# Attention scores of a batch in five PSUM jobs instead of six, with the plan of ten steps dealt anew, in a fused sparse-attention and mish kernel

## The chip, the cores and the metric

The kernel runs on 1 core of one Trainium2 chip. The metric is device time in microseconds (us), lower is better. The kernel before takes 282.59 us in the median of 3 runs (282.14 to 286.71). The execution that was profiled took 283.31 us, of which the profile's span covers 281.5 us.

## What is computed

Eight batches of 576 positions go through eight heads of 64 each, four with a local mask (the last 32 positions), four with a strided mask (every 32nd position back). The result, 4608 tokens by 512, then goes through two matrix products of 512x2048 and 2048x512 with a mish between them.

```python
scores = scale * np.matmul(q, k.transpose(0, 1, 3, 2))
mask_local = (rel >= 0) & (rel < stride)
mask_strided = (rel >= 0) & (pos[None, :] % stride == pos[:, None] % stride)
...
attn = attn / (np.sum(attn, axis=-1, keepdims=True) + 1e-09)
return np.matmul(attn, v).astype(np.float32)
...
h = x @ w_in
sp = np.where(h > 20.0, h, np.log1p(np.exp(np.minimum(h, 20.0))))
g = h * np.tanh(sp)
return (g @ w_out).astype(np.float32)
```

## The kernel before, in words

**The parts.** The tokens are taken in nine blocks of 512. From block 1 on, and for most of block 0's first product too, each matrix product is done as seven products of half size with sums of inputs and outputs (Strassen's way). A block's first product runs in four groups g of 512 features, each with the seven products `1:g` to `7:g` of four matmuls (128x128 weights, 256 columns); its second product has seven products in two halves each, `m1:0`, `m1:1` to `m7:1`, of eight such matmuls. Between them stand copies out of PSUM (`1c`, `5c`, `m1c`, `m5c`, `m6c`, `m4c`, on ScalarE when the word ends in A and on VectorE when it ends in D), VectorE's additions (`6c`, `7c`, `m3c`, `m7c`), the mish (`Z`, `E`, `H` on ScalarE), the input sums `x:0` to `x:3` (L115, tile xs, from tile xT) and the sums of the mish's output `n`, `g:1` to `g:3` (tile gs), all on VectorE.

**Attention.** A batch's scores come in units, 12 local ones (`l`, 96 queries by 128 keys) and 16 strided ones (`s`, 72 by 72), each for two inner indices e. Units are put together into jobs of two PSUM banks, one bank for each e: `q` computes the scores of a job (L261), `e` applies the exponential into SBUF (L264 to 271; one ACTIVATE where the two banks lie side by side, two where they don't), `k` multiplies by the mask on VectorE (L273), `v` multiplies by the values (L299) and `r` normalises (reciprocal and product, L304 to 318). Before the change there are three local jobs of 4 units and three strided ones of 6, 6 and 4 (L230, L231), each in a pair of banks of its own.

**PSUM.** Eight banks: SET0 and SET1 of two banks, EE0 and EE1 of one, AT of two. Blocks take SET and EE by turns for the two products; attention uses AT ("A" in the plan's words), EE0 with EE1 ("G"), or one bank of a SET with an EE ("F", "H").

**What sets the order.** Nothing is scheduled by a tool: ten strings of words, PLANS (L732 to 833), are walked from left to right (`do`, L621; `go`, L728), and each engine gets its instructions in the order in which the words issue them. So a word's place sets its place in the queue of its engine alone. Semaphores make an instruction wait for what it reads and for the readers of what it overwrites. `@b` names a batch; `^` and `_` in front of a word mean the next and the last block. Step t (one string) does block t's first product, block t-1's second, and the attention of batch t+1. Step 0 also starts up: loads, attention of batches 0 and 1, and block 0 in plain products (`p1`, `p2`, matmuls of 512 columns).

**Transfers.** GpSimd's queue issues the loads (`ld`), and words `hold` (L683) make it wait until a transposing DMA has landed. SyncE's queue issues the transposing DMAs: `D` (q and k of a batch, from batch 3 on), `y` (the local half of the attention's result into xT, L321) and `V`, and the stores `st` and `w`. Batches 0 to 2 are transposed on TensorE instead (`T`, L199) and copied by `t`; `X`, `Y` and `xc`, `yc` do the same for the result.

## Time and profile before

| | |
|---|---|
| median of 3 runs | 282.59 us |
| profiled execution | 283.31 us |
| its span | 281.5 us |
| step 0 (start, loads, batches 0 and 1) | 0 to 56.0 us of the span |
| step 1, step 2 | to 75.2, to 102.6 us |
| steps 3, 4, 5, 6 | to 132.1, 160.7, 189.6, 216.9 us |
| steps 7, 8, 9 (no attention left) | to 242.5, 265.2, 277.5 us |
| granted TensorE clock | 1.00 throughout |

How to read it: a profile row of a timeline has start, time, engine, source line, operation, tiles written and read, shape and count, and in brackets the idle time of the engine before it and what ended that. PE is TensorE's matmul side, PEld its weight loads, ACT is ScalarE, DVE VectorE, POOL GpSimd; SPq and ACTq are queues that issue DMAs. Matmuls follow each other before the earlier ones end, so a row of eight lasts longer than eight times their spacing, and TensorE's loss shows in the distance between starts rather than in its busy share.

### The profile page before, as it was taken

The page shows a single profiled execution, that of the slowest core. Times are in us where ns is not written, and L with a number is a line of the kernel's source. Part 1 is how long each engine was busy: PE and PEld are TensorE (multiplying, and loading weights), DVE is VectorE, ACT ScalarE, POOL GpSimd, SP SyncE. Part 2 cuts the span into 40 slices and gives each one's busy share as a digit, 9 for nine tenths or more (in the row PEclk, how much of TensorE's full clock was granted, in tenths as well). Part 3 has the DMA queues.
Part 4 walks back from the last instruction along what each step waited for, and adds up shares of the span by engine and source line. Part 5 has one row for each costly group of instructions (what it writes and reads, how often), then busy time and mean ns, then how long its engine had stood idle before and what let it go on. Part 6 is the DMA issues. An engine that isn't in the chain of part 4 may idle for free.

```text
span 281.5 us, 7627 instructions
## 1 busy us (share of the span) xinstructions
PE 273.5 (97%) x3235; PEld 226.1 (80%) x3241; DVE 225.4 (80%) x384; ACT 186.1 (66%) x288; POOL 57.2 (20%) x78
## 2 busy tenths in 40 slices
PE   8899999999999999999999999999999999999994
PEld 3656845679888887889898888898989888888883
DVE  4679878899899895999789969889889957837761
ACT  2575984699777787569766986679488217624830
POOL 8533421250019005400720072001000000000000
PEclk9999999999999999999999999999999999999999
DMA  7999999999929978999899899998444003002104
GB/s 148 182 205 203 204 185 191 131 229 117 169 45 118 138 140 172 194 127 160 165 194 130 164 194 166 122 154 200 62 165 68 9 2 149 2 3 98 53 0 149
DMA packets 98242, 37.35 MB, mean 133 GB/s; under 512 B 79800, under 2 KB 93688, under 8 KB 98208
## 3 DMA queue, kind: packets, MB, share of 16 engines
q0 software_dynamic: 57808, 18.30, 63.3%
q1 hardware_dynamic: 40112, 18.32, 29.2%
q8 instruction: 25, 0.41, 0.6%
q10 hardware_dynamic: 288, 0.25, 0.3%
q14 instruction: 9, 0.07, 0.1%
HBM read 37.05 MB, written 9.44 MB: 165 GB/s over the span
## 4 chain that ended last, share of the span: by engine, by line
PE 86%; DMA 6%; DVE 3%; ACT 2%; POOL 1%; issue 1%; SPq 0%; ACTq 0%; DVEq 0%; POOLq 0%
PE set L121 52%; PE ee L121 20%; PE at L121 7%; PE at L299 4%; DMA vl<-in_v_dram 4%; DMA qTs<-qs 2%; PE at L346 1%; PE ee L346 1%; DVE xs L115 1%; DVE wos L115 0%; DVE gs L115 0%; DVE osb L112 0%; DVE xT L112 0%; ACT gT L450 0%; ACT Pl L269 0%
## 5 line engine op out<-in xcount | busy, mean ns | idle before, releaser
L121 PEld LDWEIGHTS <-wis 128*128 128x128 bf16 x577 | 55.7, 99 | 10.7 <-issue 2.4
L121 PEld LDWEIGHTS <-gs 128*128 128x128 bf16 x512 | 49.0, 98 | 6.7 <-issue 0.5
L121 PEld LDWEIGHTS <-gT 128*128 128x128 bf16 x448 | 42.1, 98 | 9.4
L121 PEld LDWEIGHTS <-w_in 128*128 128x128 bf16 x436 | 40.7, 97 | 7.3 <-DMA w_in<-in_moe_w_in_dram 0.7
L121 PE MATMUL set<-w_out,gT 128*128 128x256 bf16 (+1 forms) x299 | 46.1, 294 | 0.2
L121 PE MATMUL set<-xT,w_in 128*128 128x256 bf16 (+1 forms) x263 | 40.2, 275 | 0.4 <-ACT gT L450 0.2
L450 ACT ACTIVATE gT<-set 128x1024 bf16<-128x1024 f32 x32 | 32.8, 1025 | 8.9 <-PE set L121 8.5
L121 PE MATMUL set<-xs,wis 128*128 128x256 bf16 x256 | 38.4, 273 | 0.0
L110 ACT COPY set<-set 128x512 f32<-128x512 f32 x35 | 20.2, 576 | 16.3 <-PE set L121 14.9
L121 PE MATMUL set<-wos,gs 128*128 128x256 bf16 x224 | 28.0, 273 | 0.0
L115 DVE TENSOR_TENSOR hh<-set,hh 128x512 f32<-128x512 f32 x32 | 21.9, 685 | 5.3 <-PE set L121 4.9
L115 DVE TENSOR_TENSOR ee<-set,hh 128x512 f32<-128x512 f32 x32 | 22.3, 696 | 3.8 <-PE set L121 1.7
L448 ACT ACTIVATE gT<-hh 128x512 bf16<-128x512 f32 x35 | 22.0, 635 | 4.0 <-DVE hh L115 3.7
L115 DVE TENSOR_TENSOR gs<-gT,gs 128x2048 bf16<-128x2048 bf16 x16 | 19.5, 1220 | 3.6 <-ACT gT L448 1.8
L446 ACT ACTIVATE gT<-ee 128x512 bf16<-128x512 f32 x35 | 20.1, 595 | 2.0 <-PE ee L121 2.0
L121 PE MATMUL ee<-xs,wis 128*128 128x256 bf16 x140 | 20.9, 273 | 0.0
L121 PE MATMUL ee<-xT,wis 128*128 128x256 bf16 x140 | 20.8, 272 | 0.0
L110 ACT COPY hh<-ee 128x512 f32<-128x512 f32 x20 | 11.7, 585 | 12.5 <-PE ee L121 12.5
L115 DVE TENSOR_TENSOR gs<-gT 128x2048 bf16<-128x2048 bf16 x16 | 19.5, 1218 | 0.2 <-ACT gT L448 0.2
L316 DVE TENSOR_TENSOR x_s<-at,rden 72x768 bf16<-72x768 f32 (+1 forms) x22 | 18.8, 856 | 0.8
L121 PE MATMUL set<-xs,w_in 128*128 128x256 bf16 x128 | 19.2, 272 | 0.0
L121 PE MATMUL ee<-wos,gT 128*128 128x256 bf16 x128 | 16.1, 273 | 0.0
(145 smaller groups left out, 453.0 us busy)
## 6 DMA issues: line engine op xcount, KB each, us to landing
out_dram<-osb SPq DMA_DIRECT2D x17, 512.0 KB, 3.8
vl<-in_v_dram POOLq DMA_DIRECT2D x8, 288.0 KB, 12.6
w_out<-in_moe_w_out_dram POOLq DMA_DIRECT2D x4, 512.0 KB, 15.2
ks<-in_k_dram POOLq DMA_DIRECT2D x7, 288.0 KB, 11.6
qs<-in_q_dram POOLq DMA_DIRECT2D x7, 288.0 KB, 10.3
vraw<-in_v_dram POOLq DMA_DIRECT2D x7, 288.0 KB, 7.3
w_in<-in_moe_w_in_dram POOLq DMA_DIRECT2D x3, 512.0 KB, 15.5
kl<-in_k_dram POOLq DMA_DIRECT2D x10, 144.0 KB, 9.6
```

The source lines that it names most:

```text
L110: Sc.copy(out_, in_)
L115: eng.tensor_tensor(out=out_, in0=a, in1=b, op=op)
L121: PE.matmul(o, lhsT=lhsT, rhs=rhs, start=start, stop=stop, skip_group_check=True)
L299: PE.matmul(po[:, e, i, :] if kind == "l" and self.apart else po[:, (n - n0) // per, (n - n0) % per, :], lhsT=pt[0:r, c0:c0 + 128], rhs=rh ...
L316: Dv.tensor_tensor(out=xo, in0=po[0:m, :, :, 0:D], in1=rd.unsqueeze(3).to_broadcast([m, nb, per, D]), op=ALU.mult,)
L346: PE.transpose(tr[:, n * j:n * j + n], x[0:n, u:u + 2, :].rearrange("p u d -> p (u d)"), ident[0:n, 0:n],)
L446: Sc.activation(o[:, 0:2, 256:512], two(E), AF.Mish)
L448: Sc.activation(o[:, 2:4, 256:512], two(h[:, 1, :]), AF.Mish)
L450: Sc.activation(o[:, :, 0:256].rearrange("p (b u) n -> p b u n", b=2), pair[:, 0:2, :].rearrange("p b (u n) -> p b u n", u=2), AF.Mish,)
```

## The change

The jobs of a batch are cut otherwise: strided 2, 7 and 7 units, local 5, 5 and 2. A new function `first` gives the first strided job an offset of two local units, so that the job of 2 strided units and the job of 2 local units can stand side by side in one pair of banks (columns 0 to 191 and 192 to 335 of each). From batch 2 on they do, and the batch's scores take five pairs instead of six; batches 0 and 1 keep six. The exponential keeps one call for each of the two small jobs. The sizes of the SBUF tiles and their cleared tails follow. The strings of PLANS are all written anew from the point in step 0 where batch 0's attention ends: the same words in other places, 18 of them moved from ScalarE to VectorE and 21 the other way. The rows of GpSimd's and SyncE's queues keep their order.

```diff
-    P_s = [sb([PN, 2, n * PN + 56], f"Ps{i}") for i, n in enumerate((6, 6, 4))]
-    P_l = [sb([128, 2, n * WQ + 32], f"Pl{i}") for i, n in enumerate((4, 4, 4))]
+    P_s = [sb([PN, 2, n * PN + 56], f"Ps{i}") for i, n in enumerate((2, 7, 7))]
+    P_l = [sb([128, 2, n * WQ + 32], f"Pl{i}") for i, n in enumerate((5, 5, 2))]
...
-                "s": [S_UNITS[0:6], S_UNITS[6:12], S_UNITS[12:16]],
-                "l": [L_UNITS[0:4], L_UNITS[4:8], L_UNITS[8:12]],
+                "s": [S_UNITS[0:2], S_UNITS[2:9], S_UNITS[9:16]],
+                "l": [L_UNITS[0:5], L_UNITS[5:10], L_UNITS[10:12]],
...
+        def first(self, kind, i):
+            return 2 * WQ if kind == "s" and i == 0 else 0
+
...
-            o = 0
+            o = self.first(kind, i)
             for x, y in self.parts[kind][i]:
...
-            o = len(self.parts[kind][i]) * (WQ if kind == "l" else PN)
+            c, o = len(self.parts[kind][i]) * (WQ if kind == "l" else PN), self.first(kind, i)
...
-                Sc.activation(pt[0:n, :, 0:o], ps[0:n, :, 0:o], AF.Exp, scale=scale)
+                Sc.activation(pt[0:n, :, 0:c], ps[0:n, :, o:o + c], AF.Exp, scale=scale)
...
-                "m1:1 m1c:A g:1 ae g:2 m5:0 m2:0 x:0 q:l0:A e:l0:A q:l1:F m2:1 m6:0 e:l1:F q:s0:F e:s0:F sh:D q:l2:A "
+                "g:1 m5:0 _Z:3 m5:1 m1c:D _xc:1:A:A@3 m6:0 q:l0:A q:l1:F x:0 m2:0 m2:1 _st:1 ae _ld:kl@5 e:l1:F sh:A "
```

What that moves, at three places.

ScalarE in step 3, from the table load ahead of the exponentials of batch 4 to the last of them (Pl is a local job, Ps a strided one; at_106 is the pair A, set0_102 with ee0_104 the pair F). Before:

```order
L688 ACT_TABLE_LOAD
L271 ACTIVATE Pl0_88<-at_106 128x2x384
L269 ACTIVATE Pl1_89<-set0_102 128x384
L269 ACTIVATE Pl1_89<-ee0_104 128x384
L269 ACTIVATE Ps0_85<-set0_102 72x432
L269 ACTIVATE Ps0_85<-ee0_104 72x432
L271 ACTIVATE Pl2_90<-at_106 128x2x384
L269 ACTIVATE Ps2_87<-set0_102 72x288
L269 ACTIVATE Ps2_87<-ee0_104 72x288
L271 ACTIVATE Ps1_86<-at_106 72x2x432
```

With the change:

```order
L691 ACT_TABLE_LOAD
L272 ACTIVATE Pl1_89<-set0_102 128x480
L272 ACTIVATE Pl1_89<-ee0_104 128x480
L110 COPY vl0_79<-vl0_79 32x4x5x64
L274 ACTIVATE Pl0_88<-at_106 128x2x480
L274 ACTIVATE Ps0_85<-at_106 72x2x144
L274 ACTIVATE Pl2_90<-at_106 128x2x192
L272 ACTIVATE Ps2_87<-set0_102 72x504
L272 ACTIVATE Ps2_87<-ee0_104 72x504
L274 ACTIVATE Ps1_86<-at_106 72x2x504
```

The first strided job went from the pair F to the pair A beside the last local one, its exponential stands ahead of that one's, and the copy of shared values (`sh`) came from VectorE to ScalarE.

VectorE in step 3, around the sums x:1 and x:2 (xs read from xT; xT's local half is written by the DMAs `y`), g:3 (gs) and m7c (osb). Before:

```order
L277 TENSOR_TENSOR Pl1_89<-Pl1_89,consts_sb_72 128x2x384
L115 TENSOR_TENSOR xs_63<-xT_62,xs_63 128x512
L115 TENSOR_TENSOR xs_63<-xT_62 128x512
L115 TENSOR_TENSOR gs_64<-gT_71,gs_64 128x2048
L115 TENSOR_TENSOR osb_1970<-set1_103,o5_66 128x2x256
L277 TENSOR_TENSOR Ps0_85<-Ps0_85,consts_sb_72 72x2x432
```

With the change:

```order
L115 TENSOR_TENSOR gs_64<-gT_71,gs_64 128x2048
L280 TENSOR_TENSOR Pl1_89<-Pl1_89,consts_sb_72 128x2x480
L280 TENSOR_TENSOR Pl0_88<-Pl0_88,consts_sb_72 128x2x480
L280 TENSOR_TENSOR Ps2_87<-Ps2_87,consts_sb_72 72x2x504
L115 TENSOR_TENSOR osb_1951<-set1_103,o5_66 128x2x256
L280 TENSOR_TENSOR Ps1_86<-Ps1_86,consts_sb_72 72x2x504
L280 TENSOR_TENSOR Pl2_90<-Pl2_90,consts_sb_72 128x2x192
L115 TENSOR_TENSOR xs_63<-xT_62 128x512
L115 TENSOR_TENSOR xs_63<-xT_62,xs_63 128x512 x2
```

The two sums stood ahead of g:3 and m7c; now they stand five rows behind m7c's masks, and m7c has no row that reads xT ahead of it since x:0.

TensorE at the two ends of block 0's second product. Its first matmuls (p2, 128x512), before:

```order
L208 MATMUL at_106<-consts_sb_72,kl_75 64x96
L121 LDWEIGHTS gT_71
L121 MATMUL set1_103<-w_out_59,gT_71 128x512
L121 LDWEIGHTS gT_71
L121 MATMUL set1_103<-w_out_59,gT_71 128x512
```

and with the change:

```order
L208 MATMUL at_106<-consts_sb_72,kl_75 64x96
L121 LDWEIGHTS gT_71
L121 MATMUL set0_102<-w_out_59,gT_71 128x512
L121 LDWEIGHTS gT_71
L121 MATMUL set0_102<-w_out_59,gT_71 128x512
```

The first rows of 512 columns go to SET0 now, the pair that group 3's mish (Z:3) has just read; before they went to SET1. And the first matmul of step 1's product 1:0, also into SET0, before:

```order
L121 MATMUL set1_103<-qTs_83,kTs_84 128x72
L121 LDWEIGHTS kTs_84
L121 MATMUL ee1_105<-qTs_83,kTs_84 128x72
L121 LDWEIGHTS w_in_58
L121 MATMUL set0_102<-xT_62,w_in_58 128x256
```

and with the change:

```order
L208 MATMUL ee1_105<-consts_sb_72,kl_75 64x96
L121 LDWEIGHTS w_in_58
L121 MATMUL set0_102<-xT_62,w_in_58 128x256
L121 LDWEIGHTS kTl_82
L121 MATMUL set1_103<-qTl_81,kTl_82 128x96
```

A job of scores (the six-unit s0) stood between the last transpose and 1:0; now 1:0 follows the transposes at once and the first score job, l0, comes behind it.

More of the change, by code (lines that the diff above doesn't have):

```diff
@@ L236, in __init__ @@
             }
+        def first(self, kind, i):
+            return 2 * WQ if kind == "s" and i == 0 else 0
         def bias(self, kind, i, ps):
-            nu = len(self.parts[kind][i])
+            nu, o = len(self.parts[kind][i]), self.first(kind, i)
             m, w, bm = (128, WQ, loc_b) if kind == "l" else (PN, PN, stm_b)
@@ L242, in bias @@
                 mm(
-                    (ps[e] if isinstance(ps, tuple) else ps[:, e])[:, 0:nu * w].rearrange("p (u c) -> p u c", u=nu), ident[0:m, :],
+                    (ps[e] if isinstance(ps, tuple) else ps[:, e])[:, o:o + nu * w].rearrange("p (u c) -> p u c", u=nu), ident[0:m, :],
                     bm.unsqueeze(1).to_broadcast([m, nu, w]), True, False,
@@ L268, in exp @@
                 for e in range(2):
-                    Sc.activation(pt[0:n, e, 0:o], ps[e][0:n, 0:o], AF.Exp, scale=scale)
+                    Sc.activation(pt[0:n, e, 0:c], ps[e][0:n, o:o + c], AF.Exp, scale=scale)
             else:
-                Sc.activation(pt[0:n, :, 0:o], ps[0:n, :, 0:o], AF.Exp, scale=scale)
+                Sc.activation(pt[0:n, :, 0:c], ps[0:n, :, o:o + c], AF.Exp, scale=scale)
         def mask(self, kind, i, meng):
@@ L603, in clear @@
             Dv.memset(kTs[:, 16 * SU:], 0.0)
-            for p, n in zip(P_s, (6, 6, 4)):
+            for p, n in zip(P_s, (2, 7, 7)):
                 Dv.memset(p[:, :, n * PN:], 0.0)
             Dv.memset(kTl[:, 0:32], 0.0)
-            for p in P_l:
-                Dv.memset(p[:, :, 4 * WQ:], 0.0)
+            for p, n in zip(P_l, (5, 5, 2)):
+                Dv.memset(p[:, :, n * WQ:], 0.0)
         def plain1(fc, to, ccs):
@@ L740 @@
                 "sh:D@0 b:l1:A@0 q:l1:A:b@0 X:0:e@0 e:l1:A@0 q:l0:C:b@0 wi:1536:2048 xc:0:e:D@0 ld:ks@1 X:1:f@0 "
[16 rows of a table removed]
-            ),
-            (
[6 rows of a table removed]
-            ),
-            (
[10 rows of a table removed]
-            ),
-            (
[8 rows of a table removed]
-            ),
-            (
[8 rows of a table removed]
-            ),
-            (
[7 rows of a table removed]
-            ),
-            (
[7 rows of a table removed]
-            ),
-            (
[5 rows of a table removed]
-            ),
-            (
[4 rows of a table removed]
-            ),
-            (
-                "m1:1 m1c:1:D _3:3 _E:3 m1c:0:D m5:0 m5:1 _4:3 g:1 m6:0 g:2 m6:1 _Z:3 m2:0 m5c:A m6c:1:D m7:1 m6c:0:A "
-                "m7c:1 g:3 m2:1 z:b:A w:b:S m3:1 m7:0 m7c:0 m3:0 m3c m4:1 m4:0 z:0:A z:1:A st:1 w:0:S w:1:A "
[15 rows of a table added]
+            ),
+            (
[7 rows of a table added]
+            ),
+            (
[9 rows of a table added]
+            ),
+            (
[8 rows of a table added]
+            ),
+            (
[8 rows of a table added]
+            ),
+            (
[7 rows of a table added]
+            ),
+            (
[7 rows of a table added]
+            ),
+            (
[5 rows of a table added]
+            ),
+            (
[4 rows of a table added]
+            ),
+            (
+                "m1:1 _H:3 m1c:0:D m5:0 _4:3 m5:1 _2:3 _Z:3 g:1 m1c:1:D m6:1 g:2 m6:0 m5c:D m3:1 m2:0 m6c:0:D m6c:1:D "
+                "g:3 m7:0 _st:0 m7:1 _st:1 m2:1 z:b:A w:b:S m7c:1 m3:0 m7c:0 m4:0 m4:1 m3c z:0:A st:1 w:0:S z:1:A "
+                "w:1:A "
             ),
```

139 rows, old and new, of the table PLANS are left out of this document.

## The prediction

> **What bounds the kernel now.** I read the page's busy table first, then the chain that ended last, then busy time by step. The page's first table and its chain:
>
> ```profile
> PE 273.5 (97%) x3235; PEld 226.1 (80%) x3241; DVE 225.4 (80%) x384; ACT 186.1 (66%) x288; POOL 57.2 (20%) x78
> PE 86%; DMA 6%; DVE 3%; ACT 2%; POOL 1%; issue 1%; SPq 0%; ACTq 0%; DVEq 0%; POOLq 0%
> ```
>
> TensorE is busy for all but 281.5 - 273.5 = 8.0 us, and the chain is TensorE for 86%. Busy time by step (the columns are from:to, length, PE, PEld, DVE, ACT, POOL, then the granted clock, the DMA share and GB/s), for steps 2 to 5 and 7:
>
> ```profile
> 75.20:102.60 27.40, 27.40 (x361) 24.12 (x360) 25.89 (x44) 21.05 (x33) 7.44 (x9) 1.00 1.02 109
> 102.60:132.10 29.50, 28.85 (x358) 25.10 (x355) 24.86 (x41) 21.40 (x34) 7.12 (x10) 1.00 1.26 160
> 132.10:160.70 28.60, 28.60 (x358) 24.98 (x355) 24.58 (x41) 21.36 (x33) 7.10 (x9) 1.00 1.25 167
> 160.70:189.60 28.90, 28.90 (x351) 25.34 (x348) 24.70 (x41) 21.50 (x32) 7.12 (x9) 1.00 1.34 158
> 216.90:242.50 25.60, 25.60 (x236) 22.86 (x234) 19.17 (x29) 11.95 (x19) 0.00 (x0) 1.00 0.18 54
> ```
>
> In each TensorE is full while VectorE and ScalarE have room (step 2's VectorE least, 1.5 us). How full is full, the chain in order of time says:
>
> ```profile
> 143.07 2.62 PE set L121 x24
> ```
>
> 2.62/24 = 0.109 us for a matmul of 256 columns; a half (8) is 0.87, a product (4) 0.44. The change adds and removes no matmul of that kind, no transfer and no score: same words, other places. So it can take only from TensorE's waits, and add others. The waits are few, and one step holds the largest. Steps 3 and 4 run the same list of words in the plan of before, yet take 29.5 and 28.6 us; step 3, in order of time:
>
> ```profile
> 106.69 1.04 PE L121 MATMUL set<-wos,gs 128*128 128x256 bf16 x8
> 107.97 0.27 PEld L121 LDWEIGHTS <-kTs 64*128 64x128 bf16 x12 [0.53 <-issue]
> 108.00 0.19 PE L121 MATMUL set<-qTs,kTs 64*128 64x72 bf16 x1 [0.28 <-DMA qTs<-qs]
> 111.74 0.43 DVE L115 TENSOR_TENSOR xs<-xT,xs 128x512 bf16<-128x512 bf16 x1 [1.02 <-issue]
> 112.42 1.22 DVE L115 TENSOR_TENSOR gs<-gT,gs 128x2048 bf16<-128x2048 bf16 x1
> 113.39 0.53 PE L299 MATMUL at<-vl,Pl 128*128 128x65 bf16 x12
> 113.55 0.68 DVE L115 TENSOR_TENSOR osb<-set,o 128x512 f32<-128x512 f32 x1
> 114.29 0.93 PE L121 MATMUL set<-w_out,gs 128*128 128x256 bf16 x7 [0.37 <-DVE osb L115]
> ```
>
> TensorE could have gone on at 106.69 + 8 x 0.109 = 107.56 and starts q:s0 at 108.00, when the transposed queries land: 0.44. Then it waits again: v:l0's last matmul starts 0.19 before the row's end, the next could come at 113.75, and m4:0 starts at 114.29, after m7c (the osb row): 0.54. m7c is late because x:1 sat ahead of it on VectorE, idle 1.02 us. What x:1 reads, the profile of tile xT shows:
>
> ```profile
> L323 SPq DMA_TRANSPOSE xT<-x_l x2: 1267/1567/1867, 105.4 to 107.3; - x2
> DMA to landing us min/median/max: 3.2/3.8/4.3
> ```
>
> the second of the pair is issued at 107.3 and lands up to 4.3 later, 111.6, just before x:1 starts. Both waits have a transfer behind them and come in this step alone: in step 4 the DMAs have caught up.
>
> **The change part by part.** *Step 3: -0.98.* Between q:l0 and q:s0 stood m2:1 and m6:0; now m2:0, m2:1, m6:1 and m3:1, and three halves precede q:l0 instead of two (from m1 on): q:s0 comes 3 x 0.87 = 2.6 us later in TensorE's work, the transfer was 0.44 late. The two DMA queues keep their order, and what starts them (r:l1 of batch 2, behind m1c, r:l0 and g:1 as before) too, so it lands when it did. And m7c no longer stands behind x:1. The gain is 0.44 + 0.54 = 0.98. What is late next is x:1 itself, now ahead of 6:0: from m7:1 VectorE has m7c 0.68, two masks, x:2 and x:1, some 2.4 by the rows; TensorE has 5:0, 1:0, v:l0 and m4, 0.87 + 0.36 + 1.75 = 2.98. Covered by 0.5. Bounds: nothing to 0.98.
>
> *Step 0, product 1:3: -0.34.* The mish Z:1, then TensorE:
>
> ```profile
> 27.44 1.02 ACT L450 ACTIVATE gT<-set 128x1024 bf16<-128x1024 f32 x1 [1.36 <-PE set L121]
> 27.91 0.43 PE L202 MATMUL at<-consts_sb,ks 72*128 72x72 bf16 x8 [0.51 <-DMA ks<-in_k_dram]
> 28.51 0.60 PE L121 MATMUL set<-xT,w_in 128*128 128x256 bf16 x4 [0.17 <-ACT gT L450]
> ```
>
> The eight transposes take about 0.26 (0.43 less the last one's 0.17 of pipeline), so TensorE stood from 28.17 to 28.51: 0.34. Now T:ks0 (0.26) and 7:2 (0.44) stand between; 0.70 covers it. The 0.51 ahead of the transposes is a load that lands at 27.9 either way, so whatever the new order gains or loses between 21 and 27.9 (yc:0 now stands behind three sums on VectorE, up to 0.5) ends there: priced at nothing, at most 0.3 beyond it.
>
> *p2:0:0 behind Z:3: +0.45.* Before, Z:3 and the last transposes:
>
> ```profile
> 34.28 0.70 PE L208 MATMUL ee<-consts_sb,ql 96*64 96x96 bf16 x24
> 34.45 1.02 ACT L450 ACTIVATE gT<-set 128x1024 bf16<-128x1024 f32 x1
> ```
>
> Z:3 starts 0.17 after the transposes begin and takes 1.02, and nobody needed its banks. Now p2:0:0 does, after three groups of transposes. A group costs 0.26 (0.70 less 0.17 for two), three 0.78 and the switch about 0.1. Z:3 also waits for 2:3 now, and its end is 0.27 + 1.02 + 0.04 = 1.33 behind 2:3: 1.33 - 0.88 = 0.45. Bounds: 0.2 to 1.1 (no cover at all).
>
> *1:0 and q:l0 of step 1 behind oc:0: +0.57.* The copy of block 0's output and the two copies of queries behind it:
>
> ```profile
> 54.90 0.45 PE L208 MATMUL ee<-consts_sb,kl 96*64 96x96 bf16 x12
> 55.11 1.22 DVE L112 COPY osb<-set 128x1024 f32<-128x1024 f32 x1
> 56.24 1.41 DVE L112 COPY qTl<-at 128x576 bf16<-128x576 bf16 x2
> 56.42 0.61 PE L121 MATMUL set<-xT,w_in 128*128 128x256 bf16 x4
> ```
>
> oc:0 begins 0.21 after the transposes and ends at 1.43. Before, four groups of transposes and a score job filled 54.90 to 56.42, 1.52 us: no loss. Now four groups alone, 4 x 0.26 + 0.11 = 1.15, and 1:0 waits 1.43 + 0.06 - 1.15 = 0.34. Behind it q:l0 needs the first copy of queries, 1.43 + 0.7 = 2.16 after the start, and TensorE is there at 1.49 + 0.44 = 1.93: 0.23 more. Bounds: 0.2 to 1.0.
>
> *v:s2 behind r:s1 in steps 3 and 4: -0.24.* In step 3 before:
>
> ```profile
> 125.56 0.95 DVE L316 TENSOR_TENSOR x_s<-at,rden 72x768 bf16<-72x768 f32 x1
> 126.01 0.60 PE L121 MATMUL set<-xT,w_in 128*128 128x256 bf16 x4
> 126.57 0.40 PE L299 MATMUL at<-vs,Ps 72*128 72x65 bf16 x8
> ```
>
> 1:3 leaves TensorE free at 126.45, r:s1 ends at 126.51, v:s2 starts at 126.57: 0.12 lost, with three products between v:s1 and v:s2. Now there are four (0.44 more). Twice 0.12.
>
> *The tail: -0.28.* The last two halves, their copies and stores:
>
> ```profile
> 275.73 1.91 PE L121 MATMUL at<-w_out,gs 128*128 128x256 bf16 x16
> 277.67 0.65 ACT L110 COPY osb<-at 128x256 f32<-128x256 f32 x2 [3.78 <-PE at L121]
> 278.07 0.35 SPq L563 DMA_DIRECT2D out_dram<-osb  x1
> 278.35 0.37 ACTq L563 DMA_DIRECT2D out_dram<-osb  x1
> ```
>
> m4:1 came before m4:0, and z:0, first on ScalarE, waited for the last half; so both copies run after it. Now m4:0 is first, its copy runs under m4:1, and the last store leaves one copy's step earlier, 278.35 - 278.07.
>
> *The rest: nothing.* Five jobs instead of six change neither columns nor matmuls. The exponentials' cost by the rows
>
> ```profile
> L271 ACT ACTIVATE Pl<-at 128x768 bf16<-128x768 f32 x13 | 10.5, 808 | 2.4 <-PE at L121 2.2
> L269 ACT ACTIVATE Pl<-ee 128x384 bf16<-128x384 f32 x13 | 6.0, 492 | 1.1 <-PE ee L121 1.1
> ```
>
> is (808 - 492)/384 = 0.82 ns a column and 0.18 us fixed. From batch 3 on a batch has eight calls instead of nine, 0.18 us of ScalarE, which has 6 us of room a step. The runs of score jobs, at whose ends TensorE loses about 0.1, number 30 in both orders. Counting the other handoffs of steps 1 to 9 in both orders, I find some wider and some narrower, and take zero; bounds -1.2 (what TensorE loses there now) to +2.5 (five steps with a new wait of 0.5, as long as step 3's).
>
> The sum: -0.98 - 0.34 + 0.45 + 0.57 - 0.24 - 0.28 = -0.82. Against its own time the profiled execution would go from 283.31 to 282.5; it ran 0.72 above the median of the runs, and against the median of 282.59 the forecast is **281.8 us**.
>
> A rule that speaks against the change is in the Trainium skill, page "PSUM — Partial Sum Buffer", section "PSUM bank collisions raise a hardware error": two engines must not touch one bank (in the same quadrant) at once, so a guard belongs on the bank, not on the address. For the shared pair this means that l2's exponential may not start under q:s0's matmuls although their columns differ. ScalarE's new order meets it by putting s0's exponential first. By the rule l2's exponential starts a short call later, some 0.3 us by the rows above; without it, at once; the sum is -0.82 by both, as long as ScalarE is on time. No run here shows the collision.
>
> **The rivals.** *B, the gains without the new waits.* If the two new waits fall under others (Z:3 and oc:0 earlier, since their engines were relieved) the sum is -0.98 - 0.34 - 0.24 - 0.28 = -1.84, and with half of the 1.2 of small waits 282.59 - 2.44 = 280.2. For it: the rest of the plan was dealt anew as well. Against: oc:0's chain is plain arithmetic on four rows.
>
> *C, nothing is gained.* The DMA loop of steps 2 to 5 (loads, four transposes, hold) or a later wait takes up what step 3 gives; only the order changed. 282.6. Against it: step 4 with the same words is 0.9 us shorter than step 3.
>
> *D, slower: the shared pair on a late ScalarE.* q:s1 needs the pair A again after both small exponentials: 0.41 (288 columns) + 0.49 less an overlap of 0.1, and 0.1 of handoff, 0.9 us, where TensorE has one half and q:s2, about 1.1. Before, one call of 0.81 stood there. From 0.2 us of lateness on, TensorE waits. In step 3 `sh` is now in ScalarE's way, whose price as the row of step 0 gives it is
>
> ```profile
> 44.75 1.26 ACT L110 COPY vl<-vl 32x1280 bf16<-32x1280 bf16 x1 [1.19 <-DMA vl<-in_v_dram]
> ```
>
> With half of that lost in each of steps 2 to 6, 5 x 0.63 = 3.2 comes on top: 281.8 + 3.2 = 285.0, slower than before. Against it: between q:l0 and q:l2 TensorE has 3.5 us now instead of 1.9, and VectorE took m1c and m5c off ScalarE there.
>
> **How the numbers follow.** The forecast has 0.48, B 0.22, C 0.13, D 0.12, and 0.05 is left for a wait that I don't see. The range 279.9 to 284.3 us takes in C, B with nearly all of the small waits gone (282.59 - 1.84 - 0.85), and the forecast with the rest at its upper bound (281.8 + 2.5); most of D and the unseen are outside. Two per cent, about what a measurement of this kernel can tell from no change, is 5.7 us: under 276.9 nothing in the profile could pay for, since TensorE is idle for 8.0 us in all and most of that is start and end; faster 0.02. Above 288.2 lies the far end of D and most of the unseen: slower 0.05. Within 2%: 0.93.
>
> **What would show it.** Right: step 3 as long as step 4, q:s0 without a wait for qTs, m4:0 without a wait for osb; p2:0:0 starting with ScalarE's gT row as its releaser and 1:0 with DVE's osb row; the last two copies apart, one under the last half. Wrong: a wait of TensorE at q:s1 for ScalarE's Pl row in each of steps 2 to 6 (D), the same distance from step start to q:s0's transfer as before but a new wait behind it (C), or TensorE's waits between 34 and 58 us no longer than before (B).

## The result, and the profile after

The change makes the kernel slightly slower: 285.13 us in the median of 22 runs, where the kernel before takes 283.06 on the same chip; the ratio is 1.0072, 95% interval 1.0051 to 1.0093. The forecast was 281.8, so it had the wrong sign. The runs also scatter more: 283.1 to 286.7 us for the change, 282.1 to 283.7 for the kernel before. (Executions in which the chip lowered the clock or stretched the start count in the medians, but are left out of the ranges of runs and of every ratio, and the profiles of e17 and e18 are of such ones.) The profiled execution took 284.39 us, its span is 282.6, against 283.31 and 281.5 before.

The page's first table and its chain after the change:

```profile
PE 273.8 (97%) x3241; PEld 227.0 (80%) x3241; DVE 223.6 (79%) x381; ACT 189.4 (67%) x286; POOL 57.5 (20%) x78
PE 84%; DVE 6%; DMA 5%; POOL 2%; issue 1%; ACT 1%; DVEq 0%; ACTq 0%; POOLq 0%
```

TensorE is as full as before, but VectorE has 6% of the chain instead of 3%. Where that lies shows when the steps are compared at equal work. The words at a step's end differ, so the starts of the steps are set right by what crosses them (m1:0 and m1:1 are 0.87 us of TensorE each, v:l0 is 0.36, 4:3 0.44):

| stretch | change against before, us | forecast |
|---|---|---|
| steps 0 and 1 | +0.97 | +0.68 |
| step 2 | +0.16 | 0 |
| step 3 | -1.05 | -1.10 |
| step 4 | -0.14 | -0.12 |
| step 5 | +0.01 | 0 |
| step 6 | +1.12 | 0 |
| steps 7 to 9 and the tail | +0.01 | -0.28 |
| sum | +1.08 | -0.82 |

Without step 6 the changes cancel: what step 3 gives, steps 0 to 2 take.

First what came as forecast. Step 3 in order of time, the rows that answer to those of before (the halves m2:0 and m2:1, the hold that waits for the transposed queries, the first strided scores, m7c, v:l0 and m4):

```profile
107.89 1.92 PE L121 MATMUL set<-w_out,gT 128*128 128x256 bf16 x16
108.87 0.18 POOL L689 COPY hold<-qTs 1x2 bf16<-1x2 bf16 x1 [17.06 <-DMA qTs<-qs]
111.58 0.23 PE L121 MATMUL at<-qTs,kTs 64*128 64x72 bf16 x4
114.37 0.69 DVE L115 TENSOR_TENSOR osb<-set,o 128x512 f32<-128x512 f32 x1
115.05 0.53 PE L302 MATMUL at<-vl,Pl 128*128 128x65 bf16 x12
115.41 1.80 PE L121 MATMUL set<-w_out,gs 128*128 128x256 bf16 x15
```

The transposed queries land 0.9 us later than before (the hold wakes at 108.87 instead of 108.01), but q:s0 comes at 111.58 and waits for nothing; m7c ends as v:l0 starts, and m4 follows without an idle bracket. Both waits of 0.44 and 0.54 are gone.

The new waits of steps 0 and 1, p2:0:0 behind Z:3, then 1:0 behind oc:0 and q:l0 behind the copies, are where the prediction put them:

```profile
34.48 1.02 ACT L453 ACTIVATE gT<-set 128x1024 bf16<-128x1024 f32 x1 [0.39 <-PE set L121]
35.56 1.02 PE L121 MATMUL set<-w_out,gT 128*128 128x512 bf16 x4 [0.28 <-ACT gT L453]
56.88 0.60 PE L121 MATMUL set<-xT,w_in 128*128 128x256 bf16 x4 [0.17 <-DVE osb L112]
57.41 0.38 PEld L121 LDWEIGHTS <-kTl 64*128 64x128 bf16 x10 [0.21 <-ACT kTl L110]
```

From start to start TensorE loses 0.45, 0.34 and 0.23 us at them. Two more were not forecast, product 4:2 behind 7c:2 and product 7:0 of step 1 behind 6c:0, 0.46 and 0.36 from start to start:

```profile
30.02 0.60 PE L121 MATMUL set<-xs,w_in 128*128 128x256 bf16 x4 [0.30 <-DVE hh L115]
61.82 0.60 PE L121 MATMUL set<-xs,wis 128*128 128x256 bf16 x4 [0.20 <-DVE ee L115]
```

Then step 6, VectorE and the first local product with the values of batch 7 (vc:1 is the first copy xT from ks, which holds the strided result brought by the transposing DMA V; sh is the copy vl):

```profile
188.31 1.91 SPq L332 DMA_TRANSPOSE ks<-x_s  x1
194.04 0.72 DVE L112 COPY xT<-ks 128x576 bf16<-128x576 bf16 x1 [2.33 <-DMA ks<-x_s]
196.38 0.71 DVE L112 COPY xT<-ks 128x576 bf16<-128x576 bf16 x1
198.49 1.22 DVE L115 TENSOR_TENSOR gs<-gT,gs 128x2048 bf16<-128x2048 bf16 x1
200.07 0.48 DVE L112 COPY vl<-vl 32x1280 bf16<-32x1280 bf16 x1
200.61 0.46 PE L302 MATMUL at<-vl,Pl 128*128 128x65 bf16 x10 [1.24 <-DVE vl L112]
```

VectorE stands 2.33 us for V, everything behind vc:1 in its queue comes later, sh last, and v:l0 stops after two matmuls for 1.4 us from start to start. The rows of before have the same transfer and no wait:

```profile
187.31 1.95 SPq L329 DMA_TRANSPOSE ks<-x_s  x1
195.11 0.71 DVE L112 COPY xT<-ks 128x576 bf16<-128x576 bf16 x1
```

V landed at 191.8 there and the copy came 3.3 us later. That is one wait in one execution, and it accounts for the profile's 1.1 us; the median lies 2 us above. The experiments look for the rest.

### The profile page after: what moved, and what is told of

Its sections match the earlier page's. It is cut to its first block, busy times and chain, and to the rows that moved or that the text cites. A ratio compares the mean times of both kernels' runs of the same rounds, so it can differ in the third digit from the quotient of the medians.

```text
span 282.6 us, 7628 instructions
## 1 busy us (share of the span) xinstructions
PE 273.8 (97%) x3241; PEld 227.0 (80%) x3241; DVE 223.6 (79%) x381; ACT 189.4 (67%) x286; POOL 57.5 (20%) x78
## 4 chain that ended last, share of the span: by engine, by line
PE 84%; DVE 6%; DMA 5%; POOL 2%; issue 1%; ACT 1%; DVEq 0%; ACTq 0%; POOLq 0%
PE set L121 51%; PE ee L121 20%; PE at L121 7%; DMA w_in<-in_moe_w_in_dram 5%; PE at L302 4%; DVE xs L115 1%; DVE wis L115 1%; PE at L349 1%; DVE wos L115 1%; POOL w_in L173 0%; PE ee L349 0%; DVE qTl L112 0%; DVE ee L115 0%; DVE osb L112 0%; POOL vl L160 0%
## 5 line engine op out<-in xcount | busy, mean ns | idle before, releaser
L121 PE MATMUL set<-wos,gs 128*128 128x256 bf16 x224 | 27.6, 273 | 0.0
L110 ACT COPY set<-set 128x512 f32<-128x512 f32 x31 | 17.9, 579 | 9.0 <-PE set L121 8.1
L110 ACT COPY osb<-set 128x1024 f32<-128x1024 f32 (+1 forms) x8 | 7.7, 960 | 15.8 <-PE set L121 15.8
L110 ACT COPY hh<-ee 128x512 f32<-128x512 f32 x24 | 14.1, 588 | 5.9 <-PE ee L121 5.9
```

What stands on the lines that cost most here:

```text
L110: Sc.copy(out_, in_)
L121: PE.matmul(o, lhsT=lhsT, rhs=rhs, start=start, stop=stop, skip_group_check=True)
```

## The experiments

The runs in one table. Ratios are against the kernel before on the same chip, with their 95% intervals:

| run | median, us | ratio |
|---|---|---|
| the change | 285.13 | 1.0072 (1.0051 to 1.0093) |
| e1_vc_behind | 284.38 | 1.0064 (1.0033 to 1.0096) |
| e2_cut_alone | 285.97 | 1.0098 (1.0060 to 1.0136) |
| e3_step3_alone | 283.28 | 1.0023 (1.0006 to 1.0040) |
| e4_before_0_to_2 | 286.90 | 1.0118 (1.0070 to 1.0165) |
| e5_no_vs | 282.73 | 1.0007 (0.9984 to 1.0030) |
| e6_before_no_vs | 282.77 | 1.0010 (0.9996 to 1.0024) |
| e7_cover | 284.14 | 1.0048 (1.0026 to 1.0070) |
| e8_kl1_first | 285.11 | 1.0070 (1.0052 to 1.0088) |
| e9_vs_early | 282.71 | 0.9988 (0.9969 to 1.0007) |
| e10_vs_early_mended | 282.86 | 0.9994 (0.9971 to 1.0016) |
| e11_steps01_mended | 285.35 | 1.0085 (1.0054 to 1.0117) |
| e12_before_vs_early | 282.41 | 0.9976 (0.9959 to 0.9993) |
| e13_p2_swap | 286.73 | 1.0151 (1.0101 to 1.0200) |
| e14_vs_early_p2_vc | 282.46 | 0.9992 (0.9954 to 1.0030) |
| e15_before_load_more | 283.30 | 1.0019 (0.9978 to 1.0060) |
| e16_load_more | 285.62 | 1.0082 (1.0036 to 1.0127) |
| e18_before_vs_early_x | 282.16 | 0.9971 (0.9955 to 0.9987) |

### The place of one copy: e1_vc_behind

```diff
-ae vc:1:D@6 q:l1:F e:l1:F q:l0:A e:l0:A m5:1 m5c:A m6:0 m6:1 m6c:A g:2 k:l0:D vc:0:D@6
+ae q:l1:F e:l1:F q:l0:A e:l0:A m5:1 m5c:A m6:0 m6:1 m6c:A g:2 k:l0:D vc:1:D@6 vc:0:D@6
```

> The changed kernel with one word of step 6 moved: vc:1 (VectorE's copy of the strided result of batch 6, which waits for the transposing DMA V) stands behind g:2 and k:l0 instead of ahead of them. Theory 1: the change's loss is this place. VectorE stood idle 2.33 us there, and v:l0 of batch 7 waited 1.4 us for the copy sh at the end of that row of work. With g:2 (1.22) and k:l0 (0.65) done during the wait, sh ends about 1.1 to 1.4 us earlier: v:l0's wait falls under 0.3, the profiled span to about 281.3, the median from 285.1 to about 283.7, and the runs scatter less, since the landing of V no longer reaches TensorE. Theory 2, the transfers themselves are late (their loop is 0.7 to 0.9 us behind that of the kernel before from batch 3 on): the copies vc only wait elsewhere, v:l0 still waits 0.8 or more, and the median stays at 284.5 or above.

The ratio hardly moved, and theory 1 in this form fell. The profile says why. Where TensorE waited longest in it from step 1 on, in steps 4 and 5 at the first local scores, and how long VectorE's copy still kept v:l0 (columns: total us, times, longest):

```profile
PE set L121 <- DMA kTl<-kl: 1.0, 1, 1.0
PE at L121 <- DMA kTl<-kl: 1.0, 1, 1.0
PE at L302 <- DVE vl L112: 0.4, 1, 0.4
```

The wait behind vc shrank to 0.4 as expected, although V landed even later (196.7). But now the transposed keys of two batches came too late, places at which the profile of the change had shown no wait. Nothing in the edit touches steps 4 and 5: another execution, other landings. The same view of the kernel before has a single wait for a transposed tile, 0.3 us, the one of step 3 that the prediction names.

### The cut, and halves of the change: e2, e3, e4

e2_cut_alone has the new cut of lines 89, 90 and 230 to 274 and every string of before. In it some scores of batch 7 enter the product with the values ahead of their mask, since the old strings have the masks in the old jobs' order; the work is the same.

> The new cut of the jobs (strided 2, 7, 7 units, local 5, 5, 2) with the strings of the kernel before: six pairs of banks, every word where it was. Theory 1: columns, matmuls and calls are the same in number, so the time is that of the kernel before within 0.4 us (282.7 to 283.5). Rival, the cut itself costs: jobs of 480 and 504 columns give ScalarE and VectorE longer single calls than 384 and 432 (by 0.82 ns a column and row about 0.08 to 0.16 us each), and jobs that filled a handoff no longer do; with one new wait of 0.2 to 0.4 in each of steps 1 to 6 that is 284.2 to 285.4, and the change's loss would be the cut's.

It takes 285.5 to 286.2 us, with little scatter: the rival was right, and its price of 284.2 to 285.4 too low. The new jobs tie the products to more masks. The first strided product with values, v:s0, reads 6 units in each e; with the old cut they are all job s0, with the new one jobs s0 and s1. In step 2 it then waits for the mask of s1 (Ps, 72x1008):

```profile
93.47 0.28 PE L302 MATMUL at<-vs,Ps 72*128 72x65 bf16 x4
93.48 0.67 DVE L280 TENSOR_TENSOR Ps<-Ps,consts_sb 72x1008 bf16<-72x1008 bf16 x1
94.20 0.42 PE L302 MATMUL at<-vs,Ps 72*128 72x65 bf16 x8 [0.45 <-DVE Ps L280]
```

So the cut alone, with the strings of before, costs about 1%. Whether the new strings win some of it back is not shown: the change's 1.0072 lies inside the interval of e2. The loss of e2 is one of the engines' order, not of transfers: no wait of TensorE in its profile from step 1 on has a transfer behind it, and its first local scores of steps 5 and 6 start 4.3 and 4.1 us after their data landed.

e3_step3_alone edits only step 3 of the kernel before:

```diff
-q:l1:F m2:1 m6:0 e:l1:F q:s0:F ... k:l0:D m6:1 e:l2:A ... k:l1:D x:1 m5:1 x:2 ... v:l0:A m7c 5c:0:A
+q:l1:F m2:1 m6:0 m6:1 e:l1:F q:s0:F ... k:l0:D e:l2:A ... k:l1:D m5:1 ... v:l0:A m7c x:1 x:2 5c:0:A
```

> The kernel before with step 3 alone mended, old cut: the half m6:1 ahead of q:s0, and x:1 and x:2 behind m7c. Theory 1: step 3's two waits (0.44 for the transposed queries, 0.54 for m7c) are single losses and nothing takes them up again: step 3 shrinks from 29.5 to about 28.5 us and the median by 0.98, ratio about 0.9965. Rival, the gain is taken up later (by the transfers of step 4 to 6, which then come 1 us later against TensorE's work): step 3 shrinks, but the ratio is 0.9985 or above.

No gain, a small loss. The rows of step 3:

```profile
109.10 0.19 PE L121 MATMUL set<-qTs,kTs 64*128 64x72 bf16 x1 [0.84 <-DMA qTs<-qs]
111.18 0.37 PE L121 MATMUL at<-qTs,kTs 64*128 64x72 bf16 x12 [0.32 <-ACT Pl L271]
```

The queries landed at 109.0 here, 1.1 us later than in the profile of before with the same words ahead of them, so a half more in front did not cover them; and with m6:1 taken from behind q:s0, q:s1 comes too early for the exponential of l2, a wait of 0.5 of my own making. The wait at m4:0 did go. What TensorE still lost at q:s0 is 1.0 from start to start.

e4_before_0_to_2 takes steps 0 to 2 from before and steps 3 to 9 from the change.

> Steps 0 to 2 with the strings of the kernel before, steps 3 to 9 with those of the change (step 3's first words fitted to it), the new cut throughout; in steps 0 to 2 the small jobs keep pairs of their own. Theory 1: the new waits of steps 0 to 2 (1.1 us in the profiles, counted up to the start of step 3) go, and the transfers from batch 3 on start 0.7 to 0.9 earlier, so V lands earlier in step 6 and v:l0's wait falls from 1.4 to about 0.6: 285.1 - 1.1 - 0.8 = 283.2. If the place of vc:1 alone counts and not the earlier transfers, v:l0 waits 1.4 as before: 284.0. If the losses of steps 0 to 2 are not real ones (taken up by a later wait anyway), 285 or a little under.

It missed: 286.9. Steps 1 and 2 lose what e2 loses there, and the transfers did not come earlier: v:l0 of step 6 waits 1.7 us for sh, and q:l1 of step 5 0.6 for keys that landed at 164.0.

### Theory 3: cover over transfers

What e1, e3 and e4 have in common is put together from the landing times in the traces: the time from the landing of a batch's transposed local half to its first scores on TensorE, and the same for vc behind V. 0.1 or less means that they waited.

| cover, us | batch 5 | batch 6 | batch 7 | vc behind V | local half of batch 6 landed |
|---|---|---|---|---|---|
| before | 1.8 | 4.7 | 3.8 | 3.3 | 159.7 |
| the change | 1.1 | 1.8 | 2.0 | 0.1 | 160.7 |
| e1_vc_behind | 0.1 | 0.1 | 0.9 | 0.1 | 164.4 |
| e14_vs_early_p2_vc | 2.9 | 5.7 | 6.5 | 2.9 | 156.3 |

Batches 5 to 7 have their scores in steps 4 to 6. The change has the scores of steps 5 and 6 earlier in the step, and vc with them. In its profiled execution 1.8 us were left for batch 6; in e1, which differs by one word of step 6, the same transfers land 3.7 us later. Cover is not all that a time depends on: e2 has that of the kernel before and is slow all the same. The next four runs take the transfers away, or give cover back.

e5_no_vs and e6_before_no_vs leave out the loads of the strided values of batches 4 to 7, in the change and in the kernel before; these batches use the values of batch 3.

```diff
-hold:qs@4 ld:vs@4
+hold:qs@4
```

> The changed kernel without the loads of the strided values of batches 4 to 7 (those batches use the values of batch 3; all work of the engines stays). Theory 3: the loop of transfers (a batch's last transposed queries land, the hold lets the next loads go, four transposing DMAs follow) paces steps 3 to 6 nearly as slowly as TensorE does, its landings vary by 1 to 2 us between runs, and the change uses them earlier: local scores start 1.8 and 2.0 us behind the landing in batches 6 and 7 where the kernel before had 4.7 and 3.8, vc has none where it had 3.3. One load of 288 KB less in each round of the loop lets all later transfers land 2 us or more earlier: the waits at q:l of steps 4 to 6 and behind vc in step 6 go, 285.1 - 1.4 - about 0.7 = 283.0, ratio to the kernel before 1.000 to 1.003, and the runs scatter by less than 1 us. Rival, the loss is made by the engines' own order (steps 0 to 2 and the new cut) and the transfers don't matter: the ratio stays at 1.006 to 1.007.

> The kernel before without the same loads (batches 4 to 7 use the values of batch 3). Theory 3: there the transfers have 1.8 us of cover and more from batch 5 on, so nothing is gained: within 0.3 us of the kernel before, ratio 0.999 to 1.001. If transfers limited that kernel too, it gains as the changed one does: 0.5 us or more, ratio under 0.998.

Both came as theory 3 had them: the change falls from 1.0072 to 1.0007, the kernel before stays. In the profile of e5 no wait of TensorE from step 2 on has a transfer behind it, and all but one of its runs lie between 282.1 and 283.0.

e7_cover leaves nothing out and moves words of steps 4 to 6:

```diff
-q:l0:A e:l0:A g:2 k:l0:D q:l1:F e:l1:F m2:0 ... q:s1:A m5:1
+m2:0 q:l0:A e:l0:A g:2 k:l0:D q:l1:F e:l1:F ... m5:1 q:s1:A
-q:l1:F g:1 _xc:0:a:A q:l0:A m5:1 m5c:D m2:0 g:2
+g:1 _xc:0:a:A m5:1 m5c:D m2:0 q:l1:F q:l0:A g:2
-vc:1:D@6 q:l1:F e:l1:F q:l0:A e:l0:A m5:1 m5c:A ... g:2 k:l0:D vc:0:D@6 ... sh:D
+m5:1 q:l1:F e:l1:F q:l0:A e:l0:A m5c:A ... g:2 sh:D k:l0:D vc:1:D@6 vc:0:D@6
```

> The changed kernel with cover put back in steps 4 to 6 and nothing left out: in step 4 m2:0 stands ahead of q:l0 (and m5:1 ahead of q:s1), in step 5 both first local jobs stand behind m5:1 and m2:0, in step 6 m5:1 ahead of them, vc:1 behind k:l0, and sh ahead of k:l0, since its load has long landed. That gives the transfers 0.9, 1.7 and 0.9 us more, and v:l0 of step 6 no longer hangs on V. Theory 3: the profile shows no wait of TensorE over 0.4 us in steps 4 to 6 and the median falls by 1.0 to 2.0 us to 283.1 to 284.1, ratio 1.002 to 1.004, the scatter shrinks. Rival (the engines' own order): the moved jobs hand their lateness on to their exponentials and the next jobs, ratio 1.006 or above.

By the ratio a third of the loss came back, less than expected. In its profile the transfers are late again (batch 6 at 163.9, batch 7's queries at 195.1), and TensorE still waits 0.8 us from start to start at q:s2 of step 6 and 0.4 at q:s0 of step 4, for transposed queries; 0.6 at m7:0 of step 5 is for a copy on VectorE.

e8_kl1_first moves one word of step 1:

```diff
-T:ql1:a T:ql0:A _T:kl1:f@2 _oc:0:D
+_T:kl1:f@2 T:ql1:a T:ql0:A _oc:0:D
```

> The changed kernel with one word of step 1 moved: the transposes T:kl1 of batch 2 ahead of T:ql1 and T:ql0. The loads of batch 3's local keys wait for them, so the loop of transfers starts 0.5 us earlier and, if nothing else holds it, stays so: V lands 0.5 us earlier against TensorE. Theory 3: 0.3 to 0.6 us less than the change, 284.5 to 284.8, ratio 1.005. Rival (transfers don't matter, or the loop finds its own pace later): no difference, ratio 1.007.

No difference. Half a microsecond at the head of the loop is lost in its scatter: batch 6 landed at 163.3.

### The transfers made early: e9 to e12

e9_vs_early changes the order of GpSimd's queue and nothing else:

```diff
-hold@2 ... ld:vs@3
+ld:vs@3 hold@2
-hold:qs@4 ld:vs@4
+ld:vs@4 hold:qs@4
```

and so for batches 5 and 6.

> The changed kernel with nothing left out, but in GpSimd's queue the load of the strided values of batches 3 to 6 stands one place earlier, ahead of the hold that waits for the last transfer of a round. It depends on nothing that the hold waits for, and so runs beside the four transposing DMAs instead of ahead of the next round's loads. Theory 3: the loop gets shorter by what this load took (5 to 8 us from issue to landing at the head of the round), as without the load at all, where the ratio was 1.0007: about 283.0, ratio 1.000 to 1.003, no wait of TensorE for a transfer in steps 4 to 6. Rival: the load takes from the transposing DMAs beside it what it gave to the loads (the queues share their engines), the round is as long as before, ratio 1.005 to 1.007.

The whole loss is gone with nothing left out: 0.9988. A round is what GpSimd's queue repeats for each batch: loads, four transposing DMAs, hold. In rows of GpSimd, the rounds of the kernel before, then those of the change, then those of e14, which has the same early loads (vraw is the load, hold the wait for the last transposed queries of a round):

```profile
108.01 0.18 POOL L686 COPY hold<-qTs 1x2 bf16<-1x2 bf16 x1 [17.06 <-DMA qTs<-qs]
135.15 0.25 POOL L686 COPY hold<-qTs 1x2 bf16<-1x2 bf16 x1 [19.62 <-DMA qTs<-qs]
163.08 0.28 POOL L686 COPY hold<-qTs 1x2 bf16<-1x2 bf16 x1 [20.49 <-DMA qTs<-qs]
```

```profile
108.87 0.18 POOL L689 COPY hold<-qTs 1x2 bf16<-1x2 bf16 x1 [17.06 <-DMA qTs<-qs]
109.44 0.72 POOL L157 DMA_DIRECT2D vraw<-in_v_dram  x1 [0.39 <-issue]
135.74 0.18 POOL L689 COPY hold<-qTs 1x2 bf16<-1x2 bf16 x1 [19.37 <-DMA qTs<-qs]
163.79 0.18 POOL L689 COPY hold<-qTs 1x2 bf16<-1x2 bf16 x1 [20.61 <-DMA qTs<-qs]
```

```profile
107.06 1.01 POOL L689 COPY hold<-qTs 1x2 bf16<-1x2 bf16 x1 [12.23 <-DMA qTs<-qs]
119.65 0.73 POOL L157 DMA_DIRECT2D vraw<-in_v_dram  x1 [5.26 <-DVE vs L112]
132.63 0.17 POOL L689 COPY hold<-qTs 1x2 bf16<-1x2 bf16 x1 [12.25 <-DMA qTs<-qs]
158.51 0.18 POOL L689 COPY hold<-qTs 1x2 bf16<-1x2 bf16 x1 [11.74 <-DMA qTs<-qs]
```

A round from hold to hold takes 27.1 and 27.9 us in the kernel before, 26.9 and 28.1 in the change, 29.0 and 28.2 in e13 below, and 25.6 and 25.9 in e14; the other profiles with early loads have 25.2 to 27.6. So the change's loop is no slower than that of the kernel before in these profiles; its readers come earlier. TensorE needs about 28.5 for a step. A round nearly as long as a step hardly makes up for a late landing; one that is 2.6 us shorter can.

e10_vs_early_mended adds three mends to e9: in step 0 p2:0:0 and p2:0:2 change places, in step 1 6c:0 goes ahead of sp, and vc:1 and sh stand as in e7. e11_steps01_mended has the first two on the change alone.

```diff
-Z:3 p2:0:0 ae ... sw:2:0:1:D p2:0:2
+Z:3 p2:0:2 ae ... sw:2:0:1:D p2:0:0
-_st:1@3 sp:D _st:0@3 2:0 ... q:s2:A 6c:0 1:1
+_st:1@3 6c:0 sp:D _st:0@3 2:0 ... q:s2:A 1:1
```

> As the run with the early load, and with the engines' own waits of steps 0, 1 and 6 mended: p2:0:2 ahead of p2:0:0 (0.45 behind Z:3), 6c:0 ahead of sp on VectorE in step 1 (0.36 at product 7:0), vc:1 behind k:l0 and sh ahead of it in step 6. Theory 3: with the transfers out of the way such gains count, so it is 0.6 to 1.0 us faster than the run with the early load and faster than both kernels: 281.9 to 282.4, ratio 0.997 to 1.000. Rival: what is gained in steps 0 and 1 is taken up by the transfers again, equal to the run with the early load.

> The changed kernel with only the two mends in steps 0 and 1 (p2:0:2 ahead of p2:0:0; 6c:0 ahead of sp), the transfers as they were. The two waits of 0.45 and 0.36 go from the profile. Theory 3: TensorE then comes 0.8 us earlier to transfers that land when they did, and the 0.8 turns up again at the first local scores of steps 4 and 5 or behind vc in step 6: ratio 1.006 to 1.008, no gain. Rival, TensorE's waits simply add up: 0.8 us less, 284.3, ratio 1.004.

Neither gained. The mend of step 1 made a wait of its own, product 2:0 behind 6c:0:

```profile
59.40 0.60 PE L121 MATMUL set<-xT,w_in 128*128 128x256 bf16 x4 [1.16 <-DVE ee L115]
```

1.34 us from start to start, more than the 0.36 it took away. So e11 had no gain to lose and does not test what it was meant to. Its profile shows v:l0 of step 6 stopped again (2.3 us).

e12_before_vs_early is the kernel before with the early loads.

> The kernel before with the same loads (batches 3 to 6) ahead of the holds and every other word where it was. Theory 3: both waits of its step 3 have a transfer behind them (0.44 for the transposed queries, 0.54 for m7c behind x:1, which waits for y), and these land 2 us or more earlier, so step 3 becomes as long as step 4 without any new order: 0.98 us less, 281.7, ratio 0.9965. Rival, the load slows the transposing DMAs beside it: the two waits stay, ratio 0.999 to 1.001.

0.9976, and the interval lies below 1. The size is two thirds of what was expected, and in its profile step 3 still waits at q:s0 and at m4:0 (0.75 and 0.35): the early load gained less at batch 4 than at the later ones, so where the 0.24% come from is not shown. Like for like, with the early loads in both, the change is at 0.9988 and the kernel before at 0.9976: the loss against it is gone within the intervals, and no gain is seen.

### What a gain of TensorE is worth: e13, e14

e13_p2_swap is the change with p2:0:0 and p2:0:2 exchanged alone; e14_vs_early_p2_vc has that, the early loads, and vc:1 and sh as in e7.

> The changed kernel with p2:0:2 ahead of p2:0:0 in step 0 and nothing else: p2:0:2 needs no bank of Z:3, and the wait of 0.45 goes. Theory 3: TensorE comes 0.45 us earlier to transfers that land when they did, the waits at the first local scores of steps 4 and 5 and behind vc in step 6 grow by as much: the change's ratio, 1.006 to 1.008. Rival, TensorE's waits add up: 284.7 where the change has 285.1, ratio 1.0055, which this measurement can hardly tell; the profile decides, by whether the sum of TensorE's waits in steps 3 to 6 is larger by about 0.45 than without the swap.

> The changed kernel with the loads of the strided values (batches 3 to 6) ahead of the holds, p2:0:2 ahead of p2:0:0, and in step 6 vc:1 and sh as in the run with cover. Theory 3: with the transfers early the swap's 0.45 us counts in full: 0.4 to 0.5 less than with the early load alone (ratio 0.9988), so 0.997, about 282.0, faster than both kernels. If the ratio is 0.9985 or above, gains of TensorE in step 0 are lost elsewhere than in the transfers.

e13 is slower than the change, 1.0151 (each against the kernel before on its own chip), which neither theory had. The wait behind Z:3 is gone, and TensorE waits for what transfers had to bring in three places of this execution: q:l1 of step 5, v:l0 of step 6, and 1:1 of step 3, where the copy m4c waits for a store that had not let go of its tile:

```profile
118.69 1.01 ACT L110 COPY osb<-set 128x1024 f32<-128x1024 f32 x1 [1.44 <-DMA out_dram<-osb]
119.76 0.49 PE L121 MATMUL set<-xT,w_in 128*128 128x256 bf16 x3 [1.01 <-ACT osb L110]
```

TensorE's losses in steps 3 to 6, from start to start, are 6.9 us in it against 3.7 in the change: larger by 3.1, not by 0.45. That the gain of 0.45 did not turn up in the time is shown; that it made the loss larger is not, since landings differ by that much between executions. e14 has 2.3 us in the same steps and no wait for a transfer there, but its ratio, 0.9992, is no better than that of e9: with four runs the interval is too wide to see 0.45 us.

### The same load more in both: e15, e16

```diff
+        if b == 4:
+            Po.dma_start(spare[0:PN], v[b, 4:8].rearrange("h (p j) d -> p h j d", j=CS))
```

> The kernel before with one load more: the strided values of batch 4 are loaded a second time into a tile that nobody reads, at the head of the round of batch 5. By the rows without these loads one costs a round about 2 us, so all transfers from batch 5 on land 2 us later. Theory 3: the kernel before has 1.8 us of cover in step 4, 4.7 and 3.8 in steps 5 and 6, and 3.3 behind V, so it loses 0.2 to 0.6 us: ratio 1.001 to 1.002. Rival, late transfers cost any order the same: 1.006 or more.

> The changed kernel with the same load more. Theory 3: it has 1.1 us of cover in step 4, 1.8 and 2.0 in steps 5 and 6, none behind V, so it loses most of the 2 us: 286.5 to 287.5, ratio 1.012 to 1.016, and its distance to the kernel before grows from 2 to about 4 us. Rival: it loses what the kernel before loses, the distance stays 2 us.

Inconclusive. e15 came as expected, with runs spread from 282.2 to 284.5. e16 did not: 1.0082 where theory 3 had 1.012 to 1.016, and the distance between the two ratios stayed what it is without the load (0.0063 against 0.0072), as the rival had it; the upper end of its interval just reaches 1.012. The round with the load took 29.3 us in e16 against 26.9 in the change, but in e13 it took 29.0 without the load. Rounds scatter as much as the load costs, and with so few runs these two decide nothing.

### Two terms by themselves: e17, e18

e17_tail is the change with z:0 ahead of m4:1 in the last step; it has two executions and no ratio, and serves for its order of rows alone.

> The changed kernel with the word z:0 ahead of m4:1 in the last step, nothing else. Both halves of m4 lie in one tile of two banks. Theory T: what an instruction waits for follows the order of the words for the whole tile, so z:0, which stands behind m4:1, waited for m4:1; standing ahead of it, it starts some 0.2 us after the last matmul of m4:0 starts and runs under m4:1, or, if m4:1 in its turn now waits for z:0's reading, m4:1 starts about 0.5 us later and the span grows by 0.2 to 0.4. Rival: z:0 is tied by something else (ScalarE's own queue, the store) and still starts after the last half.

Theory T holds. In the change, then in e17 (the last two halves and their two copies):

```profile
276.80 1.91 PE L121 MATMUL at<-w_out,gs 128*128 128x256 bf16 x16
278.74 0.65 ACT L110 COPY osb<-at 128x256 f32<-128x256 f32 x2 [2.03 <-PE at L121]
```

```profile
282.02 1.04 PE L121 MATMUL at<-w_out,gs 128*128 128x256 bf16 x8
283.09 0.37 ACT L110 COPY osb<-at 128x256 f32<-128x256 f32 x1 [1.16 <-PE at L121]
283.51 1.03 PE L121 MATMUL at<-w_out,gs 128*128 128x256 bf16 x8 [0.46 <-ACT osb L110]
284.58 0.37 ACT L110 COPY osb<-at 128x256 f32<-128x256 f32 x1 [1.12 <-PE at L121]
```

Behind both halves in the words, z:0 waits for both; between them, it waits for the first, and the second half waits for it. The two halves write different banks, so it is the tile of two banks that ties them. Product 2:0 in e10 is a second case: it writes the other bank of the tile from which 6c:0 reads, and waited 1.16 us for it.

e18_before_vs_early_x is e12 with x:1 and x:2 of step 3 behind m7c.

> The kernel before with the early loads (ratio 0.9976 by themselves) and, in step 3, x:1 and x:2 behind m7c instead of ahead of it. Theory: m4:0 no longer waits for m7c behind x:1 (0.35 in the profile with the early loads, 0.54 without), and nothing else changes: 0.35 to 0.5 less, ratio 0.996, faster than both kernels. Rival: x:1 and x:2 come too late for products 6:0 and 7:0 and the wait only moves: 0.9975 or above.

0.9971, interval 0.9955 to 0.9987: faster than the kernel before and than the change, the best version found. It can't be told from e12 by the ratio, and 0.996 was expected. The profile has what the term claimed, m4:0 without a wait. Steps 3 and 4 of it, with 358 and 357 matmuls:

```profile
107.50:136.10 28.60, 28.60 (x358) 24.97 (x355) 24.78 (x41) 21.37 (x34) 7.13 (x10) 1.00 1.38 170
136.10:164.70 28.60, 28.60 (x357) 24.98 (x354) 24.58 (x41) 21.36 (x33) 7.86 (x10) 1.00 1.27 166
```

Step 3 is as long as step 4, where before it was 29.5 to 28.6. The wait at q:s0 is gone too, which the edit does not touch: the queries landed 4.9 us after the step's start here, 5.5 in the profile of e12.

## Why the prediction was wrong, point by point

- **Step 3, -0.98.** Right in the profile (-1.05 with v:s2). The reason was half right: the queries landed 0.9 us later, no more than the step itself, in that execution. That a landing is a time with a scatter of a microsecond and more was not in it; e3 lost its gain to that, and to a wait of its own.
- **Step 0, product 1:3, -0.34.** The wait went and was handed on: 4:2, two products later, waits 0.46 for 7c:2, behind the copies and sums that VectorE now has there.
- **p2:0:0 behind Z:3, +0.45; 1:0 and q:l0 behind oc:0, +0.57.** The waits came where the prediction put them, 0.45, 0.34 and 0.23 from start to start. That the figures agree so well is partly luck: the forecast's 0.45 and 0.34 stand beyond about 0.1 for the switch from transposes to products, which TensorE also takes where it waits for nothing (p2:0:2 in e13, 0.10 behind the last transposes). By that reckoning they measure 0.35 and 0.24. The 2.16 of the prediction should be 2.13, the sum of its two terms. At q:l0 the profile names ScalarE's copies of the keys as the last to come; the copy of the queries ends within 0.1 of them.
- **v:s2 in steps 3 and 4, -0.24.** Right as far as the starts at equal work tell (-0.14 in step 4, 0.07 beyond the rest in step 3).
- **The tail, -0.28.** Wrong: nothing came. I took the two halves for independent because their banks differ; e17 shows that the order of the words ties them through their tile.
- **The rest: nothing.** This is the step that failed. I counted the handoffs of steps 1 to 9 in one execution and found as many wider as narrower. Of the 1.9 us by which the profiled execution misses the forecast, step 6 is 1.12, what steps 0 to 2 lose beyond it is 0.45 and the tail is 0.29. The handoffs that cost most are those from a transfer to its reader, and what counted in them was the cover left over, not whether the one profile shows a wait: 4.7 and 3.8 us at the scores of steps 5 and 6 and 3.3 behind V before, 1.8, 2.0 and none after. e5, e6 and e9 show that it is the transfers: without these loads, or with them early, the change is even with the kernel before (1.0007 and 0.9988), and the kernel before gains nothing from leaving them out. That it is the cover and nothing else about them is argued from the landings in the table; e7 gave cover back, and the third of the loss that it won lies within overlapping intervals. The median lies about 2.9 us above what the forecast made of the kernel before, 2.6 without the tail, and that is beyond the bound of +2.5 that I gave this term. The value of nothing, and with it the sign, was wrong.
- **Rivals.** C had the transfers of steps 2 to 5, but as something that takes up a gain and ends at no change; that they could turn into a loss wherever scores move towards a landing was in none of the four. B fell with the two new waits. D did not occur: q:s1 waits in no step of the change; that its 285.0 is nearly the measured time is luck. The rule of the Trainium skill on banks (page "PSUM — Partial Sum Buffer", section "PSUM bank collisions raise a hardware error") decided nothing here, as the prediction said; no run shows a collision.

What stays open: why the rounds of the change land late more often than those of before. In five of seven executions with its strings, or nearly all of them, and its loads, the local half of batch 6 landed between 163.3 and 164.7, in two at 160.7; in the three with the strings of before and all its loads at 159.7 to 161.1. The later start of the loop explains 1.1 of that at most (the local half of batch 4 landed at 104.8 in the change, at 103.8 before), and e8 (104.4) took nearly half of it away without effect. Why e13 is slower still is open too. And the forecast's 0.8 us was not seen even with the transfers out of the way: without the loads the change and the kernel before are at 1.0007 and 1.0010, with early loads at 0.9988 and 0.9976. That fits the profile, where all steps but step 6 sum to nothing.
